# Up weights on GpSimd's queue, later, in five slices that overlap by a column

## The chip, the cores and the metric

One core of one Trainium2 chip. The metric is the device time of one execution in microseconds (us), on that core. Executions of this program scatter more than most: the kernel before took between 183.05 and 192.14 us in five runs. So next to every median the range is given, and most of the argument below is read from stretches inside the profiles and not from whole times.

The profile gives each instruction a record, the stretch of time in which it ran. For a load, the record is only the issuing of it; it has landed when its data are there (0.53 us and 8.0 us in one case below). In this program SyncE, ACT (ScalarE) and GpSimd (POOL) issue the loads, each from a queue of its own.

A run counts as "slow" when it is over 1.5% above the fastest of the same kernel. Ratios of times are the mean time of one kernel's fast runs over that of the other's fast runs of the same rounds, so they are not quite the ratio of the medians quoted beside them.

## The reference

```python
def reference(A_q, A_k, A_v, A_shift_k, A_ssm_k, A_ssm_D, B_x, B_w_r, B_w_gate, B_w_up, B_w_down, c, w_mod):
    # S = 2048 tokens, D = 640, F = 1728, bf16
    x = A_q
    sa, ca, ga, sb, cb, gb = ...            # six vectors of D from silu(c) @ w_mod
    h = _layernorm(x) * (1 + ca) + sa
    x = x + ga * _A_ref(h, ...)             # short convolution, then a convolution over all S by FFT
    h = _layernorm(x) * (1 + cb) + sb
    x = x + gb * _B_ref(h, ...)
    return x

def _B_ref(x, w_r, w_gate, w_up, w_down):
    r = x @ w_r                             # one score for each token
    idx = jnp.argsort(-r, axis=-1)[:, :8]   # the 8 best tokens
    ...
    g = _silu(x_sel @ w_gate)               # only these 8 go through the MLP
    u = x_sel @ w_up
    y = g * u @ w_down
    ...                                     # times sigmoid(r), scattered back
```

The point: the MLP works on 8 tokens only, but needs all of w_gate, w_up and w_down (2.2 MB each), and it can start only when all 2048 scores are known. The weights can be loaded at any time before that.

## The kernel before

The program is written as small generators (t_P, t_AT, ...) that one string, ORDER, interleaves; the position of a token in ORDER is the position of its instructions in every engine's stream. Five blocks of 128 channels pass through the FFT; for each, U goes out to DRAM (Ud), comes back transposed (uA) and is applied to x. The parts that matter here:

```python
ORDER = """
...
BX3:2 WG H:2 WG G4 P3 H:2 LXA4 H WG:3 G4:3 LU1 BT2:2 ... P3 P4 AT0 BX4 WG:5      # the last WG:5 loads w_up
P4:3 LU2 BT3:4 AA0 BT4 AT0 BT4:3 ... AA2:2 LU3 AT3* R1 AA3 AT3* LU4
R2 AA3 GR AT4 AA4 ... R4 WD T WD BS:2 N:2 BS T F ...
"""

    def t_BT(b):                                            # U to DRAM
        ...
                if kk == 1:
                    (nc.sync if b == NB - 1 else nc.gpsimd).dma_start(out=Ud[:, 8 * hk:8 * hk + 8, :], in_=U[:])

    def t_LU(b):                                            # and back
        for hb in range(2):
            uA = ring.tile([P, 8, 256], BF, name="uA", tag="G", bufs=6)
            ...
            nc.sync.dma_start(out=uA[:], in_=src)

    def t_R(b):                                             # sums over a block, for the score and the norm
        ...
        if b == NB - 1:
            V.scalar_tensor_tensor(out=msq[:], ...)
            G.tensor_scalar(out=mu[:], in0=rsum[:, :, 2], scalar1=1.0 / D, ...)       # G is GpSimd
            G.tensor_tensor(out=r0[:], ...)
            G.tensor_scalar(out=mw[:], ...)
            G.tensor_tensor(out=r0[:], ...)

    def t_WG():                                             # gate and up weights
        for n, w_in in (("g", B_w_gate), ("u", B_w_up)):
            w_sb = W[n] = big.tile([P, NB, FFP], BF, name="w" + n, tag="A", bufs=2)
            nc.gpsimd.memset(w_sb[:, :, FF:FFP], 0.0)
            for t in range(NB):
                nc.sync.dma_start(out=w_sb[:, t, 0:FF], in_=w_in[t * P:(t + 1) * P, :])
                yield

    def t_WD():                                             # down weights, on ACT's queue
        ...
        nc.scalar.dma_start(out=wd[:, 0:7, :], ...)
        nc.scalar.dma_start(out=wd[:, 7:NFC - 1, :], ...)

    def t_T():                                              # scores, choice of tokens, MLP
        ...
        G.tensor_tensor(out=ry[:], in0=r0[:], in1=y[:], op=ALU.mult)     # n2r in the profile
        ...                                                 # then r_bf, sn (norm), top 8, MLP
```

## Time and profile before

| | before |
|---|---|
| median of the three runs given with it | 185.29 us (183.05 to 192.14) |
| the profiled run, and its span from first to last instruction | 185.92 us, 184.0 us |
| mean granted TensorE clock | 0.895 |
| GpSimd's n2r, the gate to everything after it | 154.70 us |
| from n2r to the end | 29.3 us |

Two lines of the page of the kernel before: the busy time of each engine with its share of the span, and the shares of the engines in the chain of work that ended last.

```profile
PE 148.5 (81%) x1976; PEld 117.4 (64%) x1983; DVE 151.7 (82%) x266; ACT 130.9 (71%) x142; POOL 36.9 (20%) x87
PE 43%; DMA 14%; ACT 14%; DVE 11%; issue 8%; POOL 5%; SPq 1%; POOLq 1%; ACTq 0%; DVEq 0%
```

No engine is full, and GpSimd (POOL) is 80% idle. The chain is mostly TensorE. The finer views (the chain piece by piece, SyncE's queue, waits, stretches, GpSimd's timeline) are shown in the prediction below.

### The profile page before, as it was taken

To read this page: it belongs to the slowest core of one execution; us is meant where nothing else is said; L and a number is where in the kernel's file an instruction comes from. 1 tells how busy PE (TensorE), PEld (TensorE's weight loads), DVE (VectorE), ACT (ScalarE), POOL (GpSimd) and SP (SyncE) were. 2 spreads that over 40 slices of the span, in tenths; PEclk is the share of its full clock that TensorE was granted. 3 is DMA by queue.
4 is the path that set the end of the run, shared out by engine and by line. 5 is a ranking of instruction groups with operands and counts; after the bars stand their busy time and mean duration, and the time that the engine had idled before them with its cause. 6 is when DMAs were issued, how large, how long until landed. Compare 5 with 4: busy or idle time off the path is not lost.

```text
span 184.0 us, 4708 instructions
## 1 busy us (share of the span) xinstructions
PE 148.5 (81%) x1976; PEld 117.4 (64%) x1983; DVE 151.7 (82%) x266; ACT 130.9 (71%) x142; POOL 36.9 (20%) x87
## 2 busy tenths in 40 slices
PE   7499989999959999997999669993799687377250
PEld 2257579968537978875877559873788572167140
DVE  7599789999999596699689999995559778869950
ACT  4892499996908899979779999872147645999300
POOL 8668660005000303413000100110000003200003
PEclk9969999999978999999999999999589999755555
DMA  7995989999999995999998992699995009432530
GB/s 115 140 242 150 213 239 268 165 265 274 284 391 233 335 354 176 265 257 257 266 253 271 324 327 78 192 271 383 356 297 137 4 6 330 152 142 75 217 142 2
DMA packets 68876, 40.70 MB, mean 221 GB/s; under 512 B 45112, under 2 KB 65016, under 8 KB 68856
## 3 DMA queue, kind: packets, MB, share of 16 engines
q1 hardware_dynamic: 63880, 33.99, 71.9%
q0 software_dynamic: 1232, 4.21, 6.3%
q10 hardware_dynamic: 3744, 2.22, 4.3%
q8 instruction: 15, 0.25, 0.5%
q14 instruction: 5, 0.04, 0.1%
HBM read 24.67 MB, written 10.50 MB: 191 GB/s over the span
## 4 chain that ended last, share of the span: by engine, by line
PE 43%; DMA 14%; ACT 14%; DVE 11%; issue 8%; POOL 5%; SPq 1%; POOLq 1%; ACTq 0%; DVEq 0%
PE ps L366 9%; DMA kT<-in_A_k_dram 7%; DMA uA<-Ud 6%; PE ps L385 5%; ACT A L59 5%; PE ps L345 4%; PE ps L456 3%; ACT xT L59 3%; PE ps L389 3%; PE ps L387 3%; PE p L385 2%; ACT FT L705 2%; DVE IT L715 2%; DVE IT L713 2%; PE ps L522 1%
## 5 line engine op out<-in xcount | busy, mean ns | idle before, releaser
L385 PE MATMUL ps<-A,FT 128*128 128x256 bf16 x108 | 24.7, 272 | 2.5 <-ACT A L59 2.5
L59 ACT CAST HX<-ps 128x1024 bf16<-128x1024 f32 x23 | 23.2, 1043 | 4.8 <-PE ps L389 4.8
L389 PE MATMUL ps<-A,FT 128*128 128x128 bf16 x108 | 23.6, 219 | 0.0
L387 PE MATMUL ps<-A,FT 128*128 128x128 bf16 x108 | 23.6, 219 | 0.0
L59 ACT CAST A<-ps 128x1024 bf16<-128x1024 f32 x23 | 22.5, 1059 | 0.2 <-PE ps L345 0.2
L59 ACT CAST U<-ps 128x1024 bf16<-128x1024 f32 x16 | 15.8, 1036 | 3.0 <-PE ps L423 2.8
L387 PEld LDWEIGHTS <-FT 128*128 128x128 bf16 x160 | 15.7, 98 | 3.5 <-issue 3.0
L366 PE MATMUL ps<-kT,dg 128*128 128x512 bf16 x68 | 16.5, 382 | 1.5 <-DMA kT<-in_A_k_dram 1.3
L389 PEld LDWEIGHTS <-FT 128*128 128x128 bf16 x160 | 15.7, 98 | 1.8
L385 PEld LDWEIGHTS <-FT 128*128 128x128 bf16 x160 | 15.7, 98 | 0.4
L456 PE MATMUL ps<-RAT,uA 128*128 128x128 bf16 x160 | 12.0, 237 | 4.9 <-DMA uA<-Ud 4.1
L59 ACT CAST HX<-p 128x1024 bf16<-128x1024 f32 x13 | 13.8, 1059 | 2.3 <-PE p L389 2.3
L421 PE MATMUL ps<-IT,HX 128*128 128x256 bf16 x64 | 14.6, 272 | 0.5 <-ACT A L59 0.3
L423 PE MATMUL ps<-IT,HX 128*128 128x256 bf16 x64 | 14.6, 273 | 0.3 <-DVE HX L409 0.3
L456 PEld LDWEIGHTS <-uA 128*128 128x128 bf16 x160 | 10.7, 108 | 5.4 <-DMA uA<-Ud 4.3
L366 PEld LDWEIGHTS <-dg 128*128 128x128 bf16 x80 | 7.7, 99 | 9.9 <-DMA kT<-in_A_k_dram 1.6
L427 POOL DMA_DIRECT2D Ud<-U x8 | 5.5, 691 | 42.4 <-ACT U L59 42.4
L648 DVE BATCH_NORM_STATS2 st<-xq 128x6 f32<-128x320 bf16 x32 | 13.1, 478 | 0.0
L308 POOL TENSOR_SCALAR dg<-ident,shk_f 128x128 bf16<-128x128 bf16 x16 | 10.1, 649 | 13.0 <-PE ps L366 10.1
L345 PE MATMUL ps<-RA,gA 128*128 128x256 bf16 x64 | 10.6, 312 | 2.5 <-DVE gA L352 2.3
L406 DVE TENSOR_TENSOR HX<-HX 128x2048 bf16<-128x2048 bf16 x10 | 12.2, 1225 | 0.4
L385 PE MATMUL p<-A,FT 128*128 128x256 bf16 x52 | 12.1, 272 | 0.1
(254 smaller groups left out, 386.8 us busy)
## 6 DMA issues: line engine op xcount, KB each, us to landing
uA<-Ud SPq DMA_DIRECT2D x10, 512.0 KB, 8.5
early<-in_w_mod_dram SPq DMA_DIRECT2D x6, 800.0 KB, 7.4
Ud<-U POOLq DMA_DIRECT2D x8, 512.0 KB, 7.7
gA<-in_A_ssm_k_dram SPq DMA_DIRECT2D x5, 512.0 KB, 5.8
kvd<-kvT SPq DMA_DIRECT2D x10, 256.0 KB, 3.7
xA<-kvd SPq DMA_DIRECT2D x5, 512.0 KB, 6.2
xq<-in_A_q_dram SPq DMA_DIRECT2D x4, 640.0 KB, 6.4
wg<-in_B_w_gate_dram SPq DMA_DIRECT2D x5, 432.0 KB, 4.8
```

Source lines behind the costliest of these rows:

```text
L59: self.nc.scalar.copy(out=out, in_=in_)
L308: (V if b == 0 else nc.gpsimd).tensor_scalar(out=dg[:, j, :], in0=ident[:], scalar1=shk_f[:, b, j:j + 1], scalar2=None, op0=ALU.mult)
L345: nc.tensor.matmul(ps[:, bb // 2, :, (bb % 2) * 8:(bb % 2) * 8 + 8], lhsT=src[:, 4 * g4 + bb, :], rhs=RA[:].rearrange("p k c e -> p (k c) ...
L366: nc.tensor.matmul(ps[:, i, :], lhsT=diags[b][:, j, :], rhs=kT[:, n0 - j:n0 - j + 512], start=(j == 0), stop=(j == 3))
L385: nc.tensor.matmul(ps[:, i], lhsT=FT[:, 0, k2, :], rhs=A[:, 2 * k2:2 * k2 + 2, u, :], start=True, stop=False)
L387: nc.tensor.matmul(ps[:, i, 0, :], lhsT=FT[:, 1, k2, :], rhs=A[:, 2 * k2 + 1, u, :], start=False, stop=False)
L389: nc.tensor.matmul(ps[:, i, 1, :], lhsT=FT[:, 2, k2, :], rhs=A[:, 2 * k2, u, :], start=False, stop=True)
L406: V.tensor_tensor(out=X, in0=X, in1=Hr, op=ALU.mult)
L421: nc.tensor.matmul(ps[:, i, :], lhsT=hx[:, k2, 0, 1, :], rhs=IT[:, k2, 1:3, :].rearrange("p a b -> p (a b)"), start=True, stop=False)
L423: nc.tensor.matmul(ps[:, i, :], lhsT=hx[:, k2, 1, 1, :], rhs=IT[:, k2, 0:2, :].rearrange("p a b -> p (a b)"), start=False, stop=True)
L456: nc.tensor.matmul(o, lhsT=uA[:, bb, cs * P:(cs + 1) * P], rhs=RAT[:, cs, :].rearrange("p (m e) -> p m e", e=8), start=(cs == 0), stop=(cs ...
L648: V.bn_stats(out=st1[:, m, hf, :], in_=xq[:, m, hf * 320:hf * 320 + 320])
```

## The change

Intent: take the 2.2 MB of up weights out of the crowded stretch at 115 to 139 us, where uA and Ud wait for the DMA engines, and put them into the empty one behind 140 us, on the queue of an engine that is idle there. Each slice shares one column with the one before it, so that the two writes to that column must be ordered, and a slice begins only when the last has landed: only about 432 KB are in flight at a time.

```diff
 ORDER:
-... P3 P4 AT0 BX4 WG:5
-P4:3 LU2 BT3:4 ... AA2:2 LU3 AT3* R1 AA3 AT3* LU4
+... P3 P4 AT0 BX4 P4:3
+LU2 BT3:4 ... AA2:2 LU3 AT3* R1 AA3 AT3* LU4 WG:5

     def t_WG():
-        for n, w_in in (("g", B_w_gate), ("u", B_w_up)):
-            w_sb = W[n] = big.tile([P, NB, FFP], BF, name="w" + n, tag="A", bufs=2)
-            nc.gpsimd.memset(w_sb[:, :, FF:FFP], 0.0)
-            for t in range(NB):
-                nc.sync.dma_start(out=w_sb[:, t, 0:FF], in_=w_in[t * P:(t + 1) * P, :])
-                yield
+        w_sb = W["g"] = ...                                  # gate weights as before, on SyncE
+        ...
+        w_sb = W["u"] = big.tile([P, NB, FFP], BF, name="wu", tag="A", bufs=2)
+        up = B_w_up.rearrange("(t p) f -> p t f", p=P)
+        V.memset(w_sb[:, :, FF - 1:FFP], 0.0)
+        for f0, f1 in ((1381, FF), (1035, 1382), (690, 1036), (345, 691), (0, 346)):
+            nc.gpsimd.dma_start(out=w_sb[:, :, f0:f1], in_=up[:, :, f0:f1])
+            yield
```

More of the change, by code (lines that the diff above doesn't have):

```diff
@@ L40 @@
 P2:2 BX2:2 LXA3 LK4 P2 BT1:3 LG4 MOD:2 OG G3 COL LU0 P2 X3 BT2:2 X3 COL H:2 X3 C4* H:2 X3 H BG3:4 BX3 C4 BX3 H
-BX3:2 WG H:2 WG G4 P3 H:2 LXA4 H WG:3 G4:3 LU1 BT2:2 BG4 X4:4 BG4 P3:2 H BX4:2 BG4:2 BX4 P3 P4 AT0 BX4 WG:5
-P4:3 LU2 BT3:4 AA0 BT4 AT0 BT4:3 GB AA0 AT1 AA1 AT1* AT2 R0 AA1 AT2 R0 R1* GR AA2:2 LU3 AT3* R1 AA3 AT3* LU4
+BX3:2 WG H:2 WG G4 P3 H:2 LXA4 H WG:3 G4:3 LU1 BT2:2 BG4 X4:4 BG4 P3:2 H BX4:2 BG4:2 BX4 P3 P4 AT0 BX4 P4:3
+LU2 BT3:4 AA0 BT4 AT0 BT4:3 GB AA0 AT1 AA1 AT1* AT2 R0 AA1 AT2 R0 R1* GR AA2:2 LU3 AT3* R1 AA3 AT3* LU4 WG:5
 R2 AA3 GR AT4 AA4 AT4* AA4 R2 R3 GR BS*:3 R3 R4 GR BS BS* GR:2 R4 WD T WD BS:2 N:2 BS T F BL T F N:9 T N BL
@@ L670, in t_WG @@
     def t_WG():
-        for n, w_in in (("g", B_w_gate), ("u", B_w_up)):
-            w_sb = W[n] = big.tile([P, NB, FFP], BF, name="w" + n, tag="A", bufs=2)
-            nc.gpsimd.memset(w_sb[:, :, FF:FFP], 0.0)
-            for t in range(NB):
-                nc.sync.dma_start(out=w_sb[:, t, 0:FF], in_=w_in[t * P:(t + 1) * P, :])
-                yield
+        w_sb = W["g"] = big.tile([P, NB, FFP], BF, name="wg", tag="A", bufs=2)
+        nc.gpsimd.memset(w_sb[:, :, FF:FFP], 0.0)
+        for t in range(NB):
+            nc.sync.dma_start(out=w_sb[:, t, 0:FF], in_=B_w_gate[t * P:(t + 1) * P, :])
+            yield
[4 more added lines that the diff above has]
+            nc.gpsimd.dma_start(out=w_sb[:, :, f0:f1], in_=up[:, :, f0:f1])
+            yield
     def t_WD():
```

## The prediction

> **What bounds the kernel now.** I read the page first, then the chain of work that ended last in order of time, then what SyncE's queue issued and what it waited for, then the table of stretches, then GpSimd's timeline. Up to 112 us the change touches nothing. Behind that, one piece of the chain stands out:
>
> ```profile
> 118.52 11.48 DMA uA<-Ud
> 130.00 0.05 issue
> 130.05 1.89 PE ps L456 x16
> 131.94 1.72 PE p L522 x16
> ```
>
> The columns are start, length and what. For 11.5 us the end of the kernel hangs on one transfer, the third block's uA (512 KB twice), read back from DRAM. TensorE stands idle for 4.1 us of it, because it still has older work. The issue side shows why it is late (start, length, queue, line, transfer):
>
> ```profile
> 102.68 1.36 SPq L437 DMA_DIRECT2D uA<-Ud  x2
> 115.41 2.94 SPq L675 DMA_DIRECT2D wu<-in_B_w_up_dram  x5
> 118.52 4.66 SPq L437 DMA_DIRECT2D uA<-Ud  x2
> 123.28 5.18 SPq L427 DMA_DIRECT2D Ud<-U  x2
> 128.65 8.05 SPq L437 DMA_DIRECT2D uA<-Ud  x4
> ```
>
> SyncE's queue is in order. The up weights (wu, five times 432 KB) stand ahead of the uA loads and wait until 115.41 for their buffer (the A tile of block 4, freed by TensorE's L389; the queue's own waits put 11.3 us on it). The Ud that the blocked uA load reads was sent by GpSimd at 104.63 and landed some 7.5 us later, near 112. So uA was held some 6 us in the queue and then shared the DMA engines with 2.2 MB of up weights: its halves took 11.5 and 12.6 us, where the shortest of this form took 5.3. The same crowd delays the Ud writes of block 3 (8.8 and 8.0 us), and these hold buffers:
>
> ```profile
> PE ps L456 <- DMA uA<-Ud: 4.1, 1, 4.1
> ACT t L76 <- DMA Ud<-U: 3.6, 1, 3.6
> DVE t L79 <- DMA Ud<-U: 2.2, 1, 2.2
> ```
>
> The table of stretches adds the clock (columns: PE, PEld, DVE, ACT and POOL busy, granted clock, DMA share, GB/s):
>
> ```profile
> 125.00:130.00 5.00, 0.91 (x17) 0.73 (x14) 2.43 (x4) 1.14 (x2) 0.00 (x0) 0.81 1.10 361
> 130.00:135.00 5.00, 4.95 (x48) 4.96 (x48) 2.31 (x3) 1.32 (x1) 0.00 (x0) 0.51 1.09 356
> 140.00:145.00 5.00, 4.28 (x138) 3.98 (x136) 4.36 (x7) 3.52 (x3) 0.00 (x0) 1.00 0.08 22
> 145.00:150.00 5.00, 3.48 (x172) 3.07 (x171) 4.43 (x9) 2.30 (x3) 0.00 (x0) 1.00 0.01 3
> ```
>
> DMA is full to 139 and empty from 140 to 150; the up weights are first read at 168.5. Moving them from the full stretch to the empty one is the idea, and it is sound. But the queue they move to belongs to an engine with work of its own:
>
> ```profile
> 120.63 0.53 POOL L427 DMA_DIRECT2D Ud<-U  x1 [1.59 <-ACT U L59]
> 152.88 0.26 POOL L540 TENSOR_SCALAR mu<-rsum 128x16 f32<-128x16 f32 x1 [31.71 <-DVE rsum L536]
> 153.11 0.21 POOL L541 TENSOR_TENSOR r<-rsum 128x16 f32<-128x16 f32 x1
> 154.70 0.22 POOL L731 TENSOR_TENSOR n2r<-r,n2y 128x16 f32<-128x16 f32 x1
> ```
>
> GpSimd is free for 31.7 us, then has six short operations, of which n2r (154.70) is on the chain: DVE's r_bf, the choice of tokens and the last normalisation all wait for it or follow it.
>
> **What the Trainium skill says.** (1) "DMA: Bandwidth & Descriptors", section "Issuing engines are not separate DMA queues": queues of all issuers end in the same 16 DMA engines. The trace agrees: uA went from 5.3 to 12.6 us beside the weights. So another queue gives no bandwidth; what counts is the later moment and leaving SyncE's order. (2) The same page, "Anatomy of one DMA — SWDGE (gpsimd) path", fits about 2.0 us plus bytes over 436 KB per us, 3.0 us for a slice of 444 KB. In this trace GpSimd's 512 KB writes landed after 4.9 us at best and 7.7 in the median, beside other traffic and into DRAM, so I take 3.0 as a floor. (3) "Perfetto Trace Analysis", "DMA Instruction — SWDGE (GPSIMD)": GpSimd's record ends when the last descriptor is written, not when data lands. The trace agrees: 0.53 us of record, 8.0 us to landing. (4) "TensorE: Matmul & The Clock Gate", Part 1: an idle window of about 3.4 us halves the clock. The trace agrees: after 4.1 us idle, L522's matmuls take 314 ns, 217 to 219 later.
>
> **The change, part by part.**
>
> *Removed from SyncE's queue:* five weight loads. The third uA can be issued when its Ud has landed, near 112.3, or at 114.4 if a half needs the slot of the first uA; DMA is only 0.29 busy between 110 and 115. With 5.3 to 6 us it lands by 120, before TensorE comes to it at 125.9. So that wait goes: 130.05 becomes about 125.9, 4.1 us. Without the idle gap the clock stays up: 1.89 and 1.72 us become 0.93 and 0.92 as in later rounds, another 1.8 us. That is 5.9 us. The next loads then decide: block 4's Ud leaves ACT at 125.1, lands near 131, and its uA near 137, where TensorE would have wanted it at 141.4 - 5.9 = 135.5. I let half a microsecond slip there: gain at 151.3 **about 5.4 us**, so GpSimd's mu would be wanted at 152.88 - 5.4 = 147.5.
>
> *Added on DVE:* a memset of 325 columns, an estimate of 0.3 us after GpSimd's 0.36 for 320. It stands behind the second product of block 3 (141.12 + 0.69 = 141.8 before, less 5.8, 136.0 after), and the first slice overlaps it by one column, so the first slice starts near **136.3**, as the last uA loads land.
>
> *Added on GpSimd's queue:* five slices, each with a column of the one before, so each waits for its landing. GpSimd is in order: it stands in this wait and does nothing else until the fourth has landed and the fifth is written out. A slice is 640 rows of some 692 bytes against the 128 rows of 4 KB of a Ud write, whose record is 0.53 to 0.69 us. If the time went with rows it would be 0.55 x 5 = 2.7 us a slice (upper estimate); if mostly fixed, about 1. The least loaded weight load before took 3.4 us in all (wu, first of five, on SyncE). I take **4.2 us a slice**: 3.4 plus some 0.5 for more descriptors, and 0.3 on average for the tail of the uA loads and for wd, 2.1 MB that ACT now issues near 145 instead of 150.6. Four landings are 16.8 us, the fifth's record 1.5: GpSimd is free at 136.3 + 16.8 + 1.5 = **154.6**, where it is wanted at 147.5 and was used at 152.88 before.
>
> *Sum.* mu starts 1.7 us later than before; mu to n2r was 1.8 us of back-to-back work on GpSimd and stays so; behind n2r the tail of 29 us is unchanged (the fifth slice lands near 158, wanted after 168). So the change gains 5.4 us on the uA loads and gives back 7.1 at GpSimd: **+1.7 us**. The two quicker runs before have a mean of 184.2, so I predict 186.
>
> **The rivals.** *A, the slices are quick.* At the 3.0 us floor with a record of 0.7, GpSimd is free at 136.3 + 12 + 0.7 = 149.0, and the change gains 3.9 us: 180.5. For it: DMA is almost empty from 140, and GpSimd's idle 31.7 us look as if the author had chosen them. Against it: rows of 692 bytes, and GpSimd's own writes never landed in under 4.9 us. *B, the slices are slow.* At 2.7 us of record and 1.5 to land plus contention (4.8 in all), GpSimd is free at 136.3 + 19.2 + 2.7 = 158.2: +5.3, 189.5. For it: the scatter at the end has a record of 1.60 us for few rows, and wd runs beside slices three and four. *C, no landing is waited for* (same queue, so no wait is emitted): GpSimd is free by 145 and the full 5.4 us come through, 178.8; the description of the change speaks against it. *D, the uA chain was not the bound*: the fourth and fifth uA arrive too late by as much as the third is early, the gain at 151 is only 2 us, and the slices start 3 us later too: 158 at GpSimd, 189.
>
> **Range and chances.** A shift of 1 us in a slice moves GpSimd's release by 4, so the range is wide: slices of 3.1 to 5 us give 181 to 190 around 186, and the runs before spread by over 1% themselves. Faster by over 2% needs slices under about 3.0 us or rival C: 0.22. Slower by over 2% needs slices above some 4.7 us or rival D: 0.28. Between: 0.50.
>
> **What would show each step right or wrong.** The piece of 11.5 us on uA gone from the chain, uA's transfers near 5 to 7 us, L522 on tile p at 219 ns and not 314: the first step right. The DVE memset of wu near 136, five wu transfers from GpSimd 4.2 us apart with records of 1 to 2.7 us: the size of the slices. The wait of mu for rsum gone, and DVE's n2r or ACT's first FT in the chain behind GpSimd, with wu transfers in it: the new bound. I am wrong if mu starts before 150 with DVE's rsum still its releaser (rival A or C: a clear gain), or if the first slice starts after 139 (D).

## The result and the profile after

| | before | after |
|---|---|---|
| median of five runs of the same rounds | 185.29 us (183.05 to 192.14) | 194.72 us (192.06 to 198.91) |
| ratio of the fast runs, 95% interval | | 1.0505 (1.0393 to 1.0618): slower |
| profiled run, span | 185.92 us, 184.0 us | 195.87 us, 194.1 us |

The profiled run of the kernel after is itself 2.0% above that kernel's fastest. Its granted clock is not what does it: full-speed groups take the same in both profiles (16 matmuls of L456: 1.06 or 1.07 us), and its fast runs show the loss by themselves (the lowest took 192.06 us). I use its profile for the places of things, and correct for its late start as said below.

From the page of the kernel after, the lines that answer to the two above, and its group of weight loads on GpSimd (busy time, mean ns of one, then the idle time just before them and what ended most of it):

```profile
PE 145.9 (75%) x1983; PEld 114.3 (59%) x1983; DVE 152.2 (78%) x267; ACT 130.9 (67%) x142; POOL 40.7 (21%) x91
PE 28%; DVE 24%; issue 19%; DMA 15%; POOL 6%; ACT 5%; POOLq 1%; SPq 0%; DVEq 0%
L681 POOL DMA_DIRECT2D wu<-in_B_w_up_dram x5 | 4.4, 872 | 35.5 <-DMA wu<-in_B_w_up_dram 18.8
```

Busy times hardly moved; "issue", time in which nothing that the profile shows was waited for, went from 8% to 19% of the chain. A busy table cannot show this change: GpSimd is 21% busy and bounds the kernel.

**The front half did what was wanted.** SyncE's queue after, start, length and transfers: four uA loads one behind the other with no weights ahead of them, and the last four near where they were.

```profile
104.51 10.62 SPq L437 DMA_DIRECT2D uA<-Ud  x4
127.30 6.40 SPq L437 DMA_DIRECT2D uA<-Ud  x4
```

The third block's matmuls follow the second's without a gap (three groups of 16 as one row), and uA costs TensorE 0.8 us in all against 4.1:

```profile
125.60 2.84 PE L456 MATMUL ps<-RAT,uA 128*128 128x128 bf16 x48
```

**The back half lost more.** GpSimd's timeline after; the brackets hold the idle time before a record and its releaser:

```profile
139.47 0.90 POOL L681 DMA_DIRECT2D wu<-in_B_w_up_dram  x1 [16.66 <-PE ps L456]
143.99 0.89 POOL L681 DMA_DIRECT2D wu<-in_B_w_up_dram  x1 [3.62 <-DMA wu<-in_B_w_up_dram]
148.93 0.85 POOL L681 DMA_DIRECT2D wu<-in_B_w_up_dram  x1 [4.06 <-DMA wu<-in_B_w_up_dram]
157.32 0.87 POOL L681 DMA_DIRECT2D wu<-in_B_w_up_dram  x1 [7.53 <-DMA wu<-in_B_w_up_dram]
161.81 0.85 POOL L681 DMA_DIRECT2D wu<-in_B_w_up_dram  x1 [3.63 <-DMA wu<-in_B_w_up_dram]
162.69 0.28 POOL L540 TENSOR_SCALAR mu<-rsum 128x16 f32<-128x16 f32 x1
164.52 0.22 POOL L737 TENSOR_TENSOR n2r<-r,n2y 128x16 f32<-128x16 f32 x1
```

The four brackets that name the DMA are the chain: each slice is issued when the last has landed, 4.52, 4.94, 8.39 and 4.49 us after its predecessor. (The bracket of the first slice names TensorE's L456, but what it waited for is DVE's memset: in all six profiles with slices on GpSimd the first starts 0.62 to 0.63 us after the memset's end, whenever L456 ends.) mu has no bracket any more: it starts the moment the fifth record ends, and no longer waits for DVE's rsum, which has been there long before. The chain of work that ended last says the same, piece by piece (start, length, what); the "issue" pieces are GpSimd standing in its wait for a landing:

```profile
140.37 3.61 issue
...
144.87 4.04 issue
...
149.79 7.52 issue
...
157.32 4.21 DMA wu<-in_B_w_up_dram
```

Everybody else stands. The waits (total, times, longest):

```profile
PE pq L750 <- DVE r_bf L741: 15.0, 1, 15.0
DVE n2r L740 <- POOL n2r L737: 13.8, 1, 13.8
```

And in the stretches (PE, PEld, DVE, ACT, POOL busy, granted clock, DMA share, GB/s) there are 10 us with next to nothing but DMA:

```profile
150.00:155.00 5.00, 0.32 (x2) 0.00 (x0) 0.88 (x5) 0.56 (x1) 0.00 (x0) 0.93 1.05 369
155.00:160.00 5.00, 0.00 (x0) 0.00 (x0) 0.00 (x0) 0.00 (x0) 0.87 (x1) 0.50 0.38 97
```

In the first of these rows DMA is full (1.05). That is not the up weights alone: of the down weights (wd, 2.1 MB on ACT's queue, first issued at 146.66), 1120 KB took 8.6 us and 960 KB 11.9 us. The third slice lies in the middle of them. The times of the DMA packets show how that acts: the first packet of the other four slices moves 1.6 us after the slice's start, and the last ends 3.6 to 4.2 us after it; the third slice's first packet moves only after 4.2 us and its last ends after 7.6. In its first 3.5 us all bytes that move, but for one 16 KB piece of program, are on ACT's queue, and so of wd (1.26 MB).

**A balance that the noise hardly touches.** Up to the GpSimd record that sends the second half of Ud of the third block, both kernels issue the same program. It starts at 104.63 us in the profile of before and 106.27 after; over all 13 profiles it starts between 104.6 and 112.1, and for the same kernel at 104.63 and 107.44 (before), or 109.55 and 104.70 (the same experiment twice). Much of the difference lies in loads far in front: between the two profiles of the same experiment, TensorE's waits in front of that record were 2.6 us against none for w_mod, and 2.3 against 1.1 for the transposed k. So I cut each profile in three behind that record: to DVE's first operation on the complete sums (msq, L538), from there to n2r, and from n2r to the end.

| | record to sums | sums to n2r | n2r to end | record to end |
|---|---|---|---|---|
| before | 48.18 | 1.89 | 29.30 | 79.37 |
| before, a second profile | 47.61 | 1.89 | 29.36 | 78.86 |
| after | 42.59 | 15.66 | 29.58 | 87.83 |

Against the first profile of before, the change gains 5.6 us up to the sums, loses 13.8 us from the sums to n2r, and 0.3 behind it: +8.5 us. (Against the second it gains 5.0, and the sum is +9.0.) The other 1.6 us of the 10.1 us between the two spans is the late front. 8.5 us on 184 are 4.6%, which agrees with the ratio of 1.05.

### The profile page after: what moved, and what is told of

It reads as the page before. It is cut to its first block, busy times and chain, and to the rows that moved or that the text cites. A ratio compares the mean times of both kernels' runs of the same rounds, so it can differ in the third digit from the quotient of the medians.

```text
span 194.1 us, 4718 instructions
## 1 busy us (share of the span) xinstructions
PE 145.9 (75%) x1983; PEld 114.3 (59%) x1983; DVE 152.2 (78%) x267; ACT 130.9 (67%) x142; POOL 40.7 (21%) x91
## 4 chain that ended last, share of the span: by engine, by line
PE 28%; DVE 24%; issue 19%; DMA 15%; POOL 6%; ACT 5%; POOLq 1%; SPq 0%; DVEq 0%
PE ps L366 6%; DMA kT<-in_A_k_dram 6%; DMA early<-in_w_mod_dram 5%; PE ps L385 3%; PE ps L564 3%; PE ps L345 3%; DVE T L405 2%; DMA wu<-in_B_w_up_dram 2%; DVE h L665 2%; DVE A L57 2%; PE p L385 2%; DVE HX L406 2%; POOL wu L681 2%; ACT FT L711 2%; PE ps L389 2%
## 5 line engine op out<-in xcount | busy, mean ns | idle before, releaser
L711 ACT ACTIVATE FT<-xq,sn 128x640 bf16<-128x640 bf16 x8 | 6.7, 914 | 15.2 <-DVE sn L744 15.2
L405 DVE TENSOR_TENSOR T<-HX 128x2048 bf16<-128x2048 bf16 x10 | 12.2, 1218 | 1.2 <-ACT HX L59 1.2
L681 POOL DMA_DIRECT2D wu<-in_B_w_up_dram x5 | 4.4, 872 | 35.5 <-DMA wu<-in_B_w_up_dram 18.8
```

Source lines behind the costliest of these rows:

```text
L405: V.tensor_tensor(out=T2[:], in0=X, in1=Hi, op=ALU.mult)
L711: nc.scalar.activation(out=xn(m), in_=xq[:, m, :], func=ACT.Identity, scale=rs2[:, m:m + 1], bias=nm2[:, m:m + 1])
```

## The experiments

The theory after the result (**T**): the loss is GpSimd's own order. It stands in four waits for landings, and the six short operations behind them (mu to n2r), which everything needs, stand with it. The rivals: **R1**, not the wait but the traffic: the up weights now fall together with wd and with the last blocks, and slow something that the chain needs; **R2**, descriptor work on GpSimd: five records of 640 short rows; **R3**, the later place alone would have been as bad on any queue. There is a second question: of what was the 8.4 us slice made? All experiments gave correct results. No ratio of an experiment is clear at 2%; a ratio whose interval lies below 1 is faster than before, by an amount that may be under 2%. Of the 13 profiles, those of before, e3_again, e6 and e7 are of fast runs, b0 and e5 are single runs whose state is unknown, and the other seven are of slow runs; this is one more reason to read stretches. The stretch from the record to the end repeated to 0.51 us for before, and to 0.75 for a slow and a fast run of e3. Times beside a run of the kernel before are of one session each; the table of the three stretches is the main reading for all, and the last column is to be compared with 79.4 and 78.9 (before) and 87.8 (after).

| experiment | record to sums | sums to n2r | n2r to end | record to end |
|---|---|---|---|---|
| e1_stats_on_dve | 42.87 | 2.26 | 29.82 | 74.95 |
| e2_no_chain | 45.65 | 1.90 | 29.57 | 77.12 |
| e3_chain_on_sync | 42.74 | 1.88 | 29.23 | 73.85 |
| e3_again | 43.30 | 1.88 | 29.42 | 74.60 |
| e4_only_moved | 45.46 | 1.89 | 29.26 | 76.61 |
| e5_wd_later | 43.28 | 10.13 | 29.80 | 83.21 |
| e6_two_slices | 43.02 | 1.90 | 30.25 | 75.17 |
| e7_old_place_gpsimd | 47.48 | 1.88 | 29.64 | 79.00 |
| e8_sync_wd_later | 43.37 | 1.58 | 30.04 | 74.99 |
| e9_no_chain_wd_later | 45.42 | 1.58 | 29.88 | 76.88 |

The second profile of the kernel before (b0_before_again) was taken to see how far these numbers repeat:

> The kernel before, unchanged, for a second profile. The change and the first four experiments have the same program up to the third block's write of Ud (GpSimd's fifth Ud record from the start of the tail, 104.63 us in the first profile), but reached it at 106.3 to 111.4. If that is noise of the transfers in front, this profile too reaches it anywhere from 104 to 111, and the tail behind it is 79 to 80 us as in the first profile. If the moved kernels are slowed in front by something of their own, it is reached at 104 to 105 again.

One run, 188.18 us; 78.86 us from the record to the end against 79.37. The stretches repeat to about half a microsecond where the whole span moved by 2.3.

### e1_stats_on_dve: the slices stay, the work behind them leaves GpSimd

From the kernel after; the two small operations that build the selection go too, since they also stand behind the fifth slice:

```diff
-            G.tensor_scalar(out=mu[:], in0=rsum[:, :, 2], ...)
+            V.tensor_scalar(out=mu[:], in0=rsum[:, :, 2], ...)
             (the same for r0, mw, r0, ry, E and the copy of ohC)
```

> Theory 1 (GpSimd stands in order in four waits for a landing, and the statistics behind it wait with it): with mu, r, mw, n2r, the E mask and the copy of ohC on DVE nothing on the path is left on GpSimd, though the five slices run as in the changed kernel. The gain of some 5.6 us at the end of the uA loads comes through, less about 1 us of extra DVE work: 179 to 182 us. Rival (the slices or wd arrive too late for their own readers, or their transfers slow the others): no change, 193 to 196 us, with the idle stretch of DVE before n2r still near 10 us.

Median 184.93 us (180.59 to 188.10, four runs) beside 185.18 before; ratio 0.9853 (0.9725 to 0.9982). GpSimd's slices are as slow as in the kernel after (this fourth one waits 7.26 us), but n2r is DVE's and comes first:

```profile
161.52 0.87 POOL L681 DMA_DIRECT2D wu<-in_B_w_up_dram  x1 [7.26 <-DMA wu<-in_B_w_up_dram]
166.52 0.86 POOL L681 DMA_DIRECT2D wu<-in_B_w_up_dram  x1 [4.13 <-DMA wu<-in_B_w_up_dram]
```

```profile
155.88 0.17 DVE L737 TENSOR_TENSOR n2r<-r,n2y 128x16 f32<-128x16 f32 x1
```

n2r runs 10.6 us before the fifth slice is even issued. The traffic, its time and the records are all still there, and 13.4 us of the 13.8 are gone. That speaks for T and against R1 and R2 as causes of the loss. The two fast runs took 182.33 and 180.59 us, about as expected.

### e2_no_chain: the same slices without the shared column

```diff
-        for f0, f1 in ((1381, FF), (1035, 1382), (690, 1036), (345, 691), (0, 346)):
+        for f0, f1 in ((1381, FF), (1035, 1381), (690, 1035), (345, 690), (0, 345)):
```

> The five slices do not overlap each other any more; only the first overlaps the memset. Same queue, same rows, same bytes, same starting moment. Theory 1: five records of 0.87 us back to back, GpSimd free some 5 us after the first start, mu starts when rsum is there: 178.5 to 181.5 us. Rival (software descriptors and rows of 692 bytes are the cost): mu still late by 5 us or more, 189 us or above.

Median 185.70 us (183.70 to 186.91, four runs); ratio 1.0000 (0.9890 to 1.0111). The five records follow one another, 4.33 us in all, and mu waits for DVE's rsum as before:

```profile
141.20 4.33 POOL L681 DMA_DIRECT2D wu<-in_B_w_up_dram  x5 [16.69 <-PE ps L456]
153.70 0.26 POOL L540 TENSOR_SCALAR mu<-rsum 128x16 f32<-128x16 f32 x1 [8.16 <-DVE rsum L536]
```

The 13.8 us are gone here too: five records of GpSimd work cost nothing (R2 falls), the waits between them cost it all. But the stretch to the sums is 45.65 and not 42.6 to 43.3. TensorE stands once, for no reason that the profile shows:

```profile
151.69 0.30 PE L477 MATMUL pg<-xT 128*32 128x32 bf16 x20 [2.70 <-issue]
```

That is a miss: 178.5 to 181.5 us was expected, and the fast runs took 183.70 and 184.63. So the chain of slices is good for something. That led to e8 and e9, below.

### e3_chain_on_sync and e3_again: the chain stays, on SyncE's queue

```diff
-            nc.gpsimd.dma_start(out=w_sb[:, :, f0:f1], in_=up[:, :, f0:f1])
+            nc.sync.dma_start(out=w_sb[:, :, f0:f1], in_=up[:, :, f0:f1])
```

> The chain of overlapping slices stays, but SyncE's queue stands in the waits, where nothing is due before the first store of the output. Theory 1: 179 to 182 us, slices still 4 to 8 us apart. Rival (a chain of small slices is slow wherever it is issued, and its late arrival is what costs): as the changed kernel, 193 to 196 us.

> The chain on SyncE once more, with five rounds and a second profile. Its tail from Ud to the end was 73.9 us against 79.4 before. If the front is noise of the same size in both kernels, the ratio to before over more rounds comes to 0.96 to 0.98. If the front is slower in it by itself, the ratio stays at 0.99 to 1.01 and Ud is again reached after 108 us.

The first time: median 185.81 us (181.47 to 188.75, four runs), only one of them fast, so no ratio. The second time, with five rounds: **182.27 us** (181.03 to 186.17, six runs) beside 187.31 before; ratio **0.9770 (0.9706 to 0.9833)**. Both profiles agree in the stretches (73.85 and 74.60) and differ by 4.9 us in the front; such a scatter may be why the first set of runs said nothing. From the second profile, SyncE's queue and GpSimd's mu:

```profile
136.93 20.66 SPq L681 DMA_DIRECT2D wu<-in_B_w_up_dram  x5
```

```profile
148.06 0.26 POOL L540 TENSOR_SCALAR mu<-rsum 128x16 f32<-128x16 f32 x1 [26.83 <-DVE rsum L536]
```

The queue stands in the same four waits for 20.7 us, and nothing urgent is behind it: SyncE's next job is the stores of the output. The first of them did have to wait: its data were ready at 155.84 and it went out at 157.64, right behind the fifth slice (160.13 and 164.44 in the first profile). It cost nothing, n2r to the end is 29.42 and 29.23 us against 29.30 and 29.36 before. R3 falls: the later place and the chain are both fine, on a queue behind which nobody waits for long.

### e4_only_moved: the kernel before with only the new place

The two lines of ORDER from the change, nothing else: whole rows, on SyncE, with no shared column.

```diff
-... P3 P4 AT0 BX4 WG:5
-P4:3 LU2 ... AT3* LU4
+... P3 P4 AT0 BX4 P4:3
+LU2 ... AT3* LU4 WG:5
```

> The kernel before with nothing but the place of the up loads moved behind the fifth uA load (SyncE, whole rows, GpSimd memset). If the place gives the gain of 5.6 us seen in the changed kernel up to rsum, and GpSimd alone gives it away: 178.5 to 181.5 us. If the loads now collide with the last uA loads (issued only just before): the gain is 2 to 3 us, 182 to 183 us.

Median 184.92 us (184.04 to 189.81, five runs); ratio 1.0025 (0.9943 to 1.0107). The whole time misses both expected ranges. By stretches, 2.3 to 2.8 us of the gain are there (76.61), as the second branch said, but not for its reason: TensorE waits 0.8 us for uA, no longer than in the kernel after. As in e2 all 2.2 MB go out at once, and as in e2 TensorE stands with "issue" as its releaser: 1.60 us before L522 at 150.70, whose 16 matmuls then run at half clock (1.89 us).

### e5_wd_later: the kernel after, with the down weights out of the way

```diff
-... GR:2 R4 WD T WD BS:2 N:2 BS T F ...
+... GR:2 R4 T BS:2 N:2 WD:2 BS T F ...
```

> The changed kernel with the load of wd issued behind the first normalisations on ACT instead of beside the third slice. If wd's 2.1 MB made that slice take 8.4 us, all five slices are now 4.2 to 5 us apart, GpSimd is free 3.5 to 4 us sooner and the stretch from Ud to the end falls from 87.8 to about 84 us. If the slice was slow for another reason (GpSimd's own descriptors, DVE), one slice stays at 8 us and the stretch near 88.

One run, 189.92 us. In the kernel after, one slice of the five took 8.39 us and lay beside wd. Here wd is issued behind n2r's followers, and GpSimd's third slice onward reads:

```profile
147.77 0.85 POOL L681 DMA_DIRECT2D wu<-in_B_w_up_dram  x1 [3.46 <-DMA wu<-in_B_w_up_dram]
151.84 0.87 POOL L681 DMA_DIRECT2D wu<-in_B_w_up_dram  x1 [3.21 <-DMA wu<-in_B_w_up_dram]
156.28 0.85 POOL L681 DMA_DIRECT2D wu<-in_B_w_up_dram  x1 [3.57 <-DMA wu<-in_B_w_up_dram]
```

The four intervals are 4.98, 4.35, 4.07 and 4.44 us, 17.84 in all against 22.34: 4.5 us less, and the stretch from the record to the end is 4.6 us shorter. So the long slice was wd's doing, and the rest of the loss (sums to n2r still 10.13) is the chain itself. This is one run, but e3 and e8 below are the same pair on SyncE's queue: with wd beside it, the five records of the chain span 22.47 and 20.66 us and the slowest slice lands after 9.4 and 9.7; with wd later they span 14.35, and the slowest lands after 4.8.

### e6_two_slices: one wait instead of four, still on GpSimd

```diff
-... AT3* LU4 WG:5
+... AT3* LU4 WG:2
-        for f0, f1 in ((1381, FF), (1035, 1382), (690, 1036), (345, 691), (0, 346)):
+        for f0, f1 in ((863, FF), (0, 864)):
```

> The changed kernel with two slices of 1.1 MB in place of five, still overlapping by a column and on GpSimd's queue: one wait for a landing instead of four. If standing in four waits is the cost, the first slice lands some 6 us after its start, the second's record takes 1 us, GpSimd is free 7 us after the start, just before the sums are ready: the stretch from Ud to the end is 74 to 76 us (five slices: 87.8; before: 79), and the time 2 to 3% under the kernel before. If small rows or the GpSimd queue as such were the cost, the stretch stays above 80 us.

Median **183.33 us** (182.95 to 184.21, four runs, all fast) beside 187.81 before; ratio **0.9822 (0.9761 to 0.9882)**.

```profile
139.50 0.90 POOL L681 DMA_DIRECT2D wu<-in_B_w_up_dram  x1 [15.70 <-PE ps L456]
145.79 0.89 POOL L681 DMA_DIRECT2D wu<-in_B_w_up_dram  x1 [5.39 <-DMA wu<-in_B_w_up_dram]
149.02 0.26 POOL L540 TENSOR_SCALAR mu<-rsum 128x16 f32<-128x16 f32 x1 [2.34 <-DVE rsum L536]
```

A slice of 1.1 MB takes 6.3 us, so GpSimd is free 2.3 us before it is wanted. This is the idea of the change with one number altered: it works here because the one landing waited for fits in the window. n2r to the end is 0.9 us longer than before; ACT's issue of wd takes 3.26 us in this profile, which I did not follow further.

### e7_old_place_gpsimd: the old place, the other queue

The kernel before, with only the up weights' five whole loads on GpSimd's queue, at the old place in ORDER.

```diff
-                nc.sync.dma_start(out=w_sb[:, t, 0:FF], in_=w_in[t * P:(t + 1) * P, :])
+                (nc.sync if n == "g" else nc.gpsimd).dma_start(out=w_sb[:, t, 0:FF], in_=w_in[t * P:(t + 1) * P, :])
```

> The kernel before with the up loads at their old place and moment (115 us) but from GpSimd's queue, whole rows, no chain. If the third uA was late mainly because it stood behind them in SyncE's order, it now goes out near 112 to 114, lands by 120, and most of the gain is there without moving the bytes: the stretch from Ud to the end falls from 79.4 to 75 to 77 us. If sharing the DMA engines was the cause, the third uA still lands after 126 and the stretch stays at 78 to 80 us.

Median 188.77 us (184.76 to 193.14, four runs) beside 187.31. 79.00 us from the record to the end: no gain at all, a miss for the expectation that SyncE's order was a good part of the loss before. The third uA does go out early now, in one row with the first ones, but the bytes are in the same crowd, and it meets the next block, as the chain shows:

```profile
120.80 9.62 DMA Ud<-U
...
130.56 4.20 DMA uA<-Ud
...
134.81 1.89 PE ps L456 x16
```

Ud of the fourth block takes 9.62 us beside the weights, its uA can be issued only at 130.56, and TensorE loses its clock one block later (1.89 us for a group of 16). So what the change gains comes from moving the bytes, and leaving SyncE's order by itself gained nothing here.

### e8_sync_wd_later and e9_no_chain_wd_later: what the unpaced slices do

Both with the new place of wd of e5: e8 on top of e3, e9 on top of e2. One theory of e2's 2.7 us was that all of wu and all of wd in flight together are too much; then wd later should close the gap. The other was that unpaced wu is enough.

```diff
-... GR:2 R4 WD T WD BS:2 N:2 BS T F ...
+... GR:2 R4 T BS:2 N:2 WD:2 BS T F ...
```

> The chain on SyncE with the load of wd behind the first normalisations as well, so that neither the slices nor TensorE's instruction refills meet it. If the chain is off the path on SyncE, only the half microsecond of TensorE's issue gap is left to gain: stretch from Ud to the end 73 to 74.6 us, ratio to before 0.96 to 0.98. If wd comes too late for its own product near the end, the stretch grows by 1 us or more.

> The five slices without the chain (GpSimd), with wd later. Without the chain and with wd beside it, TensorE stood 2.7 us in an issue gap with 2.2 MB of wu and 2.1 MB of wd in flight, and the stretch to the end was 77.1 us against 73.9 with the chain on SyncE. If the crowd of wu and wd held up TensorE's instruction refill, the gap shrinks below 1 us here and the stretch is 73.5 to 75 us. If the unpaced wu alone does it, the gap stays above 1.5 us.

e8: median 189.43 us (183.19 to 190.95, four runs, one of them fast, the front of its profile the latest of all at 112.1); 74.99 us in the stretches where 73 to 74.6 was expected, a miss: no better than e3, since nobody waits for the slices there. e9: 187.03 us (182.78 to 191.06, four runs); 76.88, no better than e2: TensorE stands 2.96 us with "issue" as releaser, at 153.39. The theory of wd missed; the unpaced wu is enough.

What the trace holds beside it are the packets of the instruction queue, the 16 KB pieces of program that are fetched while the kernel runs. From the packets' starts (us from the span's start):

| | two fetches one behind the other | interval | TensorE stands |
|---|---|---|---|
| e2, not paced | 142.32, 149.05 | 6.73 | 148.99 to 151.69 |
| e9, not paced | 143.77, 150.79 | 7.02 | 150.44 to 153.39 |
| e4, not paced | 141.68, 148.28 | 6.60 | 149.10 to 150.70 |
| after, paced, same piece as in e2 | 140.30, 144.59 | 4.29 | not at all |
| e3_again, paced, same piece as in e2 | 139.82, 143.50 | 3.68 | 0.67 |
| before, same piece as in e2 | 144.26, 148.52 | 4.26 | not at all |

In the ten profiles with one slice in flight at a time, or with the weights at the old place, this piece of program (fetched some 4.4 us before the sums) came 3.5 to 4.3 us after the one before it. In e2 and e9, which put 2.2 MB in flight at once in front of it, it came after 6.73 and 7.02; in e4 the piece before it was the late one (6.60, elsewhere 3.5 to 5.1). In the last 12 us before the sums TensorE stood for 2.70, 2.96 and 1.60 us at once with "issue" as releaser in these three, and nowhere for over 0.67 in the ten. It fits a fetch that queues behind bulk loads. That is three of three against none of ten, but the queueing itself was not isolated by a run, and the trace does not say which engine's program a piece is. All three profiles are of slow runs; that alone is not it, as four other profiles of slow runs (after, e1, e3, e8) show no such stand.

## Why the prediction was wrong

It said 186 us with a range of 181 to 190; the measured median is 194.72. By its own steps:

- **What bounds the kernel, and the gain on uA: right.** The third uA is issued early, its 11.5 us piece is gone from the chain, TensorE's wait for uA fell from 4.1 to 0.8 us, and L522 on tile p runs in 1.06 us and not 1.91. Predicted about 5.4 us up to the sums, measured 5.6 (48.18 to 42.59; 5.0 against the second profile of before). Its reason was half right: e7 shows that leaving SyncE's order alone gives nothing (79.00 against 79.37 and 78.86); the absence of the bytes gives it. Its reading "after 4.1 us idle" is also too simple: the granted clock fell at 128.1, when TensorE had been idle for 2.2 us. In the 3.4 us before, it had been busy for 1.21; in e7 it fell after 3.4 us with 1.19 busy, in e4 after 3.4 us with 0.55 busy, without one gap of 3.4 us.
- **GpSimd stands in its waits and becomes the bound: right**, in the form that the prediction gave it (mu's wait for rsum gone, DVE's n2r behind GpSimd, wu transfers in the chain). e1, e2, e3 and e6 each remove it in another way, and each brings the stretch from the sums to n2r back to 1.9 to 2.3 us.
- **"I take 4.2 us a slice", "Four landings are 16.8 us": the step that failed.** The four measured 22.34 us. Of the 5.5 us too few, 4.2 are the third slice (8.39 against 4.2), and wd is what made it: e5 takes wd away and the four measure 17.84. The prediction did have wd in its sum, as part of "0.3 on average"; that is 1.2 us in all for wd and for the tail of the uA loads together, where wd alone cost 4.5. The information was in the profile: wd is 2.1 MB, as much as all five slices, and the slice issued beside it moved nothing for 4.2 us where the others stood for 1.6. An average over the slices hides that one of them takes the whole hit, and in a chain each hit counts in full. The remaining 1.3 us are the undisturbed slices, 4.5 to 4.9 us against 4.2 (4.07 to 4.98 in e5).
- **The start, 136.3: 1.5 us early.** In the kernel after the first slice starts at 139.47, which is 137.8 after subtracting the 1.64 us by which that profile's front is late. DVE's product that the memset follows ends at 136.85 in that clock and not at 136.0, so the gain at this place was 5.0 us and not 5.8. The memset takes 0.33 us (0.3 predicted), and then 0.6 us pass from its end to the slice's start, which I had left out. (On SyncE's queue, in e3, e3_again and e8, the slice starts 0.02 to 0.03 us after the memset.)
- **The last record, 1.5 us: 0.6 too many.** A slice's record takes 0.85 to 0.90 us, a Ud write's 0.53. Five times the rows make it 1.6 times as long: neither of the two readings that the prediction offered for a record.
- **The sum.** 1.5 for the start, 5.5 for the landings and -0.6 for the record are 6.4 us, and GpSimd is free at 161.05 in the clock of before (162.69 - 1.64) instead of 154.6. From +1.7 that makes +8.1; the measured stretches say +8.5, the rest being 0.3 behind n2r and rounding. The two medians differ by 9.4 us and the predicted 186 misses by 8.7; of that, some 2 us belong to no step of the prediction, but to the base of 184.2, 1.1 below the median before, and to the scatter of the front.
- **The rivals.** Rival B named the right direction (slices slow, +5.3) and still had wd at a fraction of its cost. A and C are refuted by the four waits, D by the 5.0 to 5.6 us gained: its sign, a first slice after 139, did appear at 139.47, but 1.64 us of that are the late front. (A's sum is slightly off: 184.2 - 3.9 is 180.3, not 180.5.) The range came from slices of 3.1 to 5 us; the measured mean of 5.6 lies outside.

What stays open: why the fetch of instructions is late in the unpaced kernels (seen in three of three, no isolating run), and what makes the front of this program arrive anywhere within 7.5 us.

## What to carry to other kernels

A transfer that waits for another's landing costs its issuing engine the whole landing, so before such a chain goes to an idle engine, look not at how busy that engine is but at the first thing behind the chain that somebody needs, and at the number of landings that fit before it: here four did not, one did (0.982), and on a queue with nothing urgent behind it all four did (**0.977**, the lowest ratio, though its interval overlaps those of e1 and e6). Count the landings one by one against whatever else is in flight at that time; a small average allowance for contention hides the one landing that takes the whole hit. And where whole runs scatter by more than the effect, cut the profiles at a record that both kernels reach with the same program behind them, and compare the pieces.

## What the Trainium skill lacked or had wrong

- "DMA: Bandwidth & Descriptors", section "Issuing engines are not separate DMA queues", says that issuing from several engines only saves sequencer time, which is "usually small relative to the DMA itself". For independent transfers e7 agrees (79.00 us against 79.37 and 78.86). For transfers that wait for each other the choice of queue decided everything here: the same chain cost 13.8 us on GpSimd and 0.0 on SyncE. The same page's "Anatomy of one DMA — SWDGE (gpsimd) path" says that any semaphore wait is done by the issuing sequencer before dispatch, and the trace agrees (brackets of 3.6 to 7.5 us on GpSimd); what no page draws is the consequence for a load that waits, that compute behind it on the engine stands too.
- The fit of that section gives 3.0 us for 444 KB, an estimate worked out from it. Slices of 640 rows of 692 bytes followed each other after 4.07 to 4.98 us with no other bulk load in flight (e5), a slice of 1.1 MB after 6.3 us (e6; the fit gives an estimate of 4.5), and a slice beside 2.1 MB of other weights after 8.39. In e5 some 1.6 us of each interval pass before the first packet moves, 1.9 to 2.6 while packets move, and 0.7 to 0.8 from the last packet to the next slice.
- No page says how long GpSimd's record of such a transfer is by the number of rows: 0.53 us for 128 rows of 4 KB, 0.85 to 0.90 for 640 rows of 692 bytes, the same 0.90 for 640 rows of 1.7 KB.
- "Runtime: NRT & Kernel Launch", section "Instruction fetch mechanics", says that the program is fetched in 16 KiB blocks and that the cost is mostly hidden. In ten profiles without such a burst the runs agree (TensorE never stood for over 0.67 us in this stretch). With 2.2 MB put in flight at once a fetch came 6.6 to 7.0 us after the last one, and TensorE stood for 1.60, 2.70 and 2.96 us; the page has nothing on fetches that compete with bulk loads.
- "TensorE: Matmul & The Clock Gate", Part 1, does not say how much work a window may hold and still count as idle. Here the granted clock halved after 3.4 us with 0.55 (e4), 1.19 (e7) and 1.21 us (before) of TensorE busy, before any one gap had lasted 3.4 us.
